# Tap matrices from unnormalized exponentials, transposes of two halves moved, five blocks in halves: a start-up change to a convolution and feed-forward kernel

## The chip, the cores and the metric

The kernel runs on one core of one Trainium2 chip. The metric is the device time of one execution in microseconds (us). Times are medians of several executions of one compiled kernel. PE is TensorE (PEld its weight loads), DVE is VectorE, ACT is ScalarE, POOL is GpSimd, and SP is the engine that issues DMAs.

## The reference

A causal depthwise convolution with softmax weights over 7 taps, then a two-layer feed-forward with leaky ReLU:

```python
w = np.exp(weight - weight.max(-1, keepdims=True))            # [8 heads, 7 taps]
w = w / (w.sum(-1, keepdims=True) + 1e-9)
# x: [8, 4096, 192], 24 columns to a head, padded with 6 zero rows in front
y = np.einsum('hk,bskhg->bshg', w, x_unfolded)                 # the convolution
h = y.reshape(32768, 192) @ w_in                               # 192 -> 2048
out = np.maximum(0.01 * h, h) @ w_out                          # 2048 -> 192
```

## The kernel before

Two batch rows are worked on side by side. Rows are taken in blocks of 512 positions (32 blocks), and the first `NHALF` blocks are cut in two. I call the pieces half 0, half 1 and so on, in order; `groups` lists them. While PE works on one group, DVE computes the convolution of the next group (21 instructions: 3 column chunks of 7 taps). The point at which the halves end and whole blocks of 512 begin I call the change of width, and DVE's lead is how far its convolutions run ahead of PE. For halves 0 and 1 PE computes two of the three chunks itself, by multiplying with diagonal "tap matrices", one for each tap and each of two bf16 parts of the weight (high and low).

```python
groups = [(b, h * HT, HT) for b in range(NHALF) for h in range(2)]     # NHALF = 3
groups += [(b, 0, ST) for b in range(NHALF, NBLK)]
...
# start: softmax, divided first, then split in two bf16 parts, then tap matrices
nc.vector.tensor_scalar_add(rsum, wraw[:, :, K : K + 1], 1e-9)
nc.vector.reciprocal(rsum, rsum)
nc.vector.tensor_mul(wk, wraw[:, :, 0:K], rsum.to_broadcast([128, NCH, K]))
nc.vector.tensor_copy(out=wkb, in_=wk)
...
# main loop: j is a step of two units; a unit is the first matmul for 2 (or 1) of 16 F-chunks
for j in range(steps):
    for u in range(2 * j, 2 * j + 2):
        mm1(grp, u)                          # first matmul, then ACT: leaky ReLU to g
        ...
    for _ in range(quota):
        mm2_slot(slot)                       # second matmul, lagging one group behind
    ...
    if i in (1, 2) and j == 0:
        transpose_first(i + 1)               # PE: transposes of the NEXT half's x
        evac_first(i + 1, nc.vector.tensor_copy, nc.vector.tensor_copy)
    for job in ahead[per * j : per * (j + 1)]:
        job()                                # DVE: convolution of the next group
    if i == 1 and j == 3:
        for e in range(2):
            cast_first(3, e, nc.vector.tensor_copy)
```

Only the first four halves are cast and transposed on the engines like this. All later blocks are cast by the load and transposed by a DMA.

Of the kernel before, what the change touches and what calls it, by code (L numbers as in the profile page):

```python
# [9 lines left out]
FP32 = mybir.dt.float32  # L10
BF16 = mybir.dt.bfloat16
# [3 lines left out]
def kernel(  # L15
# [8 lines left out]
    nc = tc.nc  # L24

    B, S, D = x.shape
    H, K = weight.shape
# [8 lines left out]
    NCH = D // CH  # L36
    ST = 512
# [5 lines left out]
    NBLK = (B // 2) * NB  # L43
    LAG = NFC + NFC // 2
    WQ = 4
    NHALF = 3
    NPEC = 2

    const_pool = ctx.enter_context(tc.tile_pool(name="const", bufs=1))
# [51 lines left out]
    def new_xt(rp):  # L101
        xt[rp] = xt_pool.tile([128, NCH, HALO + S], BF16, name="xt")
        nc.vector.memset(xt[rp][:, :, 0:HALO], 0.0)
# [3 lines left out]
    def load_first(q):  # L107
        t = stage_pool.tile([128, 2, HS, D], FP32, name="x_nat")
        for e in range(2):
            nc.sync.dma_start(  # L110
                out=t[:, e, :, :],
                in_=x[e, q * HT : (q + 1) * HT, :].rearrange("(c p) d -> p c d", p=128),
            )
        x_nat[q] = t

    def cast_first(q, e, copy):
        if q % 2 == 0 and e == 0:
            x_bf[q // 2] = xb_pool.tile([128, NCH, SUB, 2, CH], BF16, name="x_bf")
        h = q % 2
        copy(  # L120
            out=x_bf[q // 2][:, :, h * HS : (h + 1) * HS, e, :],
            in_=x_nat[q][:, e, :, :].rearrange("p s (c k) -> p c s k", c=NCH),
        )
# [3 lines left out]
    def transpose_first(q):  # L127
        ts = [
            psum_o.tile([128, HS, NCH, CH], BF16, name=f"ptr{i}", tag="po") for i in range(2)
        ]  # L130
        for s in range(HS):
            for c in range(NCH):
                for i in range(2):
                    ps = slice(i * CH, (i + 1) * CH)
                    nc.tensor.transpose(  # L135
                        out=ts[i][:, s, c, :],
                        in_=x_bf[q // 2][ps, c, (q % 2) * HS + s, :, :].rearrange(
                            "p e k -> p (e k)"
                        ),
                        identity=ident[ps, ps],  # L140
                    )
        ptr[q] = ts

    def evac_first(q, *copies):
        dst = xt[0][:, :, HALO + q * HT : HALO + (q + 1) * HT].rearrange(
            "p c (s i k) -> p i s c k", s=HS, i=2
        )
        for i, t in enumerate(ptr.pop(q)):
            copies[i](out=dst[:, i], in_=t)  # L149


    yt = {}
# [27 lines left out]

    def pe_conv_jobs(grp, c):

        blk, t0, T = grp
        acc = psum_o.tile([128, ST], FP32, name="acc", tag="po")
        jobs = []
        for k in range(K):
            for p in range(2):
                jobs.append(
                    lambda k=k, p=p: nc.tensor.matmul(  # L189
                        out=acc[:, :T], lhsT=diag[c][:, p, k, :],  # L190
                        rhs=xt[0][:, c, BASE + k + blk * ST + t0 : BASE + k + blk * ST + t0 + T],
                        start=(k == 0 and p == 0), stop=(k == K - 1 and p == 1),
                    )
                )
        return jobs, lambda copy: copy(out=yt[blk][:, c, t0 : t0 + T], in_=acc[:, :T])  # L195


    w9 = const_pool.tile([H, K + 1], FP32, name="w9")
    nc.scalar.dma_start(out=w9[:, 0:K], in_=weight)
    load_first(0)  # L200
    load_first(1)

    zero = const_pool.tile([128, ST], BF16, name="zero")
    nc.vector.memset(zero, 0.0)  # L204
    junk = const_pool.tile([128, 1], FP32)
    nc.vector.memset(junk, 0.0)  # L206
# [26 lines left out]
    def warm(n):  # L233
        for _ in range(n):
            nc.tensor.matmul(  # L235
                out=wa[:, 0, :], lhsT=zero[:, 0:128], rhs=zero, start=True, stop=True
            )


# [7 lines left out]
        out=w9[:, 0:K], in_=w9[:, 0:K], func=mybir.ActivationFunctionType.Exp,  # L247
        bias=nmax, scale=1.0, accum_out=w9[:, K : K + 1],
    )
    warm(6)  # L250
    wps = psum_h.tile([128, 2, ST], FP32, name="wps", tag="ph")
    for c in range(NCH):
        nc.tensor.matmul(  # L253
            out=wps[:, 0, c * (K + 1) : (c + 1) * (K + 1)],
            lhsT=sel[:, c, :, :].rearrange("h e k -> h (e k)"),
            rhs=w9, start=True, stop=True,
        )
    new_xt(0)
    cast_first(0, 0, nc.vector.tensor_copy)
    cast_first(0, 1, nc.scalar.copy)  # L260
    wraw = wps[:, 0, 0 : NCH * (K + 1)].rearrange("p (c k) -> p c k", c=NCH)
    rsum = const_pool.tile([128, NCH, 1], FP32)
    nc.vector.tensor_scalar_add(rsum, wraw[:, :, K : K + 1], 1e-9)
    nc.vector.reciprocal(rsum, rsum)
    wk = const_pool.tile([128, NCH, K], FP32, name="wk")
    nc.vector.tensor_mul(wk, wraw[:, :, 0:K], rsum.to_broadcast([128, NCH, K]))

    wkb = const_pool.tile([128, NCH, K], BF16, name="wkb")
    wkp = const_pool.tile([128, 2, NCH, K], FP32, name="wkp")
    nc.vector.tensor_copy(out=wkb, in_=wk)  # L270
    nc.vector.tensor_copy(out=wkp[:, 0], in_=wkb)  # L271
    nc.vector.tensor_sub(wkp[:, 1], wk, wkp[:, 0])


    transpose_first(0)
    warm(3)
    evac_first(0, nc.vector.tensor_copy, nc.scalar.copy)
    diag = [const_pool.tile([128, 2, K, 128], BF16, name=f"diag{c}") for c in range(NPEC)]
    for p in range(2):
        nc.vector.tensor_mul(  # L280
            diag[0][:, p],
            ident[:, None, :].to_broadcast([128, K, 128]),
            wkp[:, p, 0, :, None].to_broadcast([128, K, 128]),
        )
        for k in range(K):
            nc.scalar.activation(  # L286
                out=diag[1][:, p, k, :], in_=ident,
                func=mybir.ActivationFunctionType.Copy, scale=wkp[:, p, 1, k : k + 1],
            )
    cast_first(1, 1, nc.scalar.copy)  # L290
    load_first(2)
    jobs = conv_jobs(groups[0], range(NPEC, NCH))
    for c in range(NPEC):
        pe_jobs, evac_y = pe_conv_jobs(groups[0], c)
        for job in pe_jobs:
            job()
        if c == 0:
            for job in jobs:
                job()
            evac_y(nc.vector.tensor_copy)  # L300
        else:
            evac_y(nc.scalar.copy)
    cast_first(1, 0, nc.vector.tensor_copy)
    load_first(3)
    load_x(2)
    transpose_x(2)
# [89 lines left out]
    for i, grp in enumerate(groups):  # L396
        blk, t0, T = grp
        steps = T // 64
        if t0 == 0:
            g[blk] = g_pool.tile([128, NFC, 2, ST], BF16, name="g", tag="g")  # L400
        quota = (avail - slot) // steps

        if i == 0:
            ahead, pe_ahead = [], []
        else:
            ahead = conv_jobs(groups[i + 1]) if i + 1 < len(groups) else []
        per = -(-len(ahead) // (steps - 1)) if T == ST else -(-len(ahead) // steps)
        for j in range(steps):
            for u in range(2 * j, 2 * j + 2):
                mm1(grp, u)  # L410
                if i == 0 and u == 0:
                    transpose_first(1)
                    evac_first(1, nc.vector.tensor_copy, nc.vector.tensor_copy)
                    ahead = conv_jobs(groups[1], range(NPEC, NCH))
                    evacs = []
                    for c in range(NPEC):
                        pe_jobs, evac_y = pe_conv_jobs(groups[1], c)
                        pe_ahead += pe_jobs
                        evacs.append(evac_y)
                    per = len(ahead)  # L420
                if i == 0 and u >= 2:
                    n = -(-len(pe_ahead) // (8 - u))
                    for job in pe_ahead[:n]:
                        job()
                    pe_ahead = pe_ahead[n:]
            for _ in range(quota):
                mm2_slot(slot)
                slot += 1
            if i == 0 and j == 3:
                for evac_y in evacs:  # L430
                    evac_y(nc.vector.tensor_copy)
                for e in range(2):
                    cast_first(2, e, nc.vector.tensor_copy)
            if i in (1, 2) and j == 0:

                transpose_first(i + 1)
                evac_first(i + 1, nc.vector.tensor_copy, nc.vector.tensor_copy)
            for job in ahead[per * j : per * (j + 1)]:
                job()
            if i == 1 and j == 3:  # L440
                for e in range(2):
                    cast_first(3, e, nc.vector.tensor_copy)

            last_half = t0 + T == ST
            if j == steps // 4 and last_half:
                load_x(blk + 3)
            if j == steps // 2 and last_half and blk > 0:
                transpose_x(blk + 2)
        avail += 2 * T // 128 * NFC
# [37 lines left out]
```

## Time and profile before

| | before |
|---|---|
| time, median of 3 runs | 709.54 us |
| span of the profiled execution | 708.6 us |
| PE busy, share of the span | 98% |
| PE waiting for DVE's convolution in the main loop | 6.5 us, three waits |

The profile's part on the chain of waits follows the last instruction back to whatever released it. For the kernel before, by engine:

```profile
PE 90%; DVE 8%; issue 1%; ACT 0%; ACTq 0%
```

The 8% of DVE, about 57 us, lie within the first 89 us. Behind that the profile lists no wait of PE for the convolution. The prediction below shows the lines on waits and timeline.

### The profile page before, as it was taken

The page shows a single profiled execution, that of the slowest core. Times are in us where ns is not written, and L with a number is a line of the kernel's source. Part 1 is how long each engine was busy: PE and PEld are TensorE (multiplying, and loading weights), DVE is VectorE, ACT ScalarE, POOL GpSimd, SP SyncE. Part 2 cuts the span into 40 slices and gives each one's busy share as a digit, 9 for nine tenths or more (in the row PEclk, how much of TensorE's full clock was granted, in tenths as well). Part 3 has the DMA queues.
Part 4 walks back from the last instruction along what each step waited for, and adds up shares of the span by engine and source line. Part 5 has one row for each costly group of instructions (what it writes and reads, how often), then busy time and mean ns, then how long its engine had stood idle before and what let it go on. Part 6 is the DMA issues. An engine that isn't in the chain of part 4 may idle for free.

```text
span 708.6 us, 25496 instructions
## 1 busy us (share of the span) xinstructions
PE 694.9 (98%) x11527; PEld 609.1 (86%) x11527; DVE 537.1 (76%) x970; ACT 509.2 (72%) x558; POOL 142.0 (20%) x198
## 2 busy tenths in 40 slices
PE   8979999999999999999999999999999999999997
PEld 4879967888888888888888888888888888888887
DVE  5579996777778777778877777877777877777712
ACT  5757797777777777777777777777777777777770
POOL 7431150122221122222022222112222111000000
PEclk9999999999999999999999999999999999999999
DMA  9972674555653565664455655455576355222112
GB/s 177 119 76 50 83 86 69 79 74 75 81 85 65 84 70 73 91 80 74 76 74 75 80 81 86 66 78 76 72 92 80 64 86 69 52 63 58 46 36 68
DMA packets 184845, 54.35 MB, mean 77 GB/s; under 512 B 148384, under 2 KB 184736, under 8 KB 184736
## 3 DMA queue, kind: packets, MB, share of 16 engines
q0 software_dynamic: 98768, 14.17, 29.1%
q1 hardware_dynamic: 85952, 38.56, 23.7%
q8 instruction: 90, 1.47, 0.9%
q14 instruction: 19, 0.16, 0.1%
q10 hardware_dynamic: 16, 0.00, 0.0%
HBM read 29.88 MB, written 25.17 MB: 78 GB/s over the span
## 4 chain that ended last, share of the span: by engine, by line
PE 90%; DVE 8%; issue 1%; ACT 0%; ACTq 0%
PE po L348 45%; PE ph L328 43%; DVE yt L174 7%; PE acc L189 1%; DVE yt L168 1%; PE warm L235 0%; ACT g L335 0%; DVE xt L149 0%; PE wps L253 0%; DVE diag L280 0%; PE ptr L135 0%; DVE yt L195 0%; ACT yt L195 0%; DVE o_sb L387 0%; DVE zero L204 0%
## 5 line engine op out<-in xcount | busy, mean ns | idle before, releaser
L335 ACT ACTIVATE g<-ph 128x1024 bf16<-128x1024 f32 x512 | 496.6, 1021 | 176.2 <-PE ph L328 176.2
L174 DVE SCALAR_TENSOR_TENSOR yt<-xt,wk,yt 128x512 bf16<-128x512 bf16 (+1 forms) x606 | 431.8, 713 | 15.8
L348 PEld LDWEIGHTS <-g 64*128 64x128 bf16 (+1 forms) x8048 | 375.4, 94 | 30.8 <-ACT g L335 0.4
L328 PE MATMUL ph<-yt,w_in 64*128 64x512 bf16 (+1 forms) x3360 | 394.7, 359 | 7.4 <-DVE yt L174 6.5
L348 PE MATMUL po<-w_out,g 64*128 64x192 bf16 (+1 forms) x8048 | 400.9, 243 | 0.1
L328 PEld LDWEIGHTS <-w_in 64*128 64x128 bf16 x3360 | 244.9, 94 | 55.9 <-issue 12.1
L79 POOL DMA_DIRECT2D x_bf<-in_x_dram x180 | 133.7, 772 | 444.3 <-DMA xt<-x_bf 429.4
L387 DVE COPY o_sb<-po 128x192 f32<-128x192 f32 x232 | 83.0, 358 | 135.2 <-PE po L348 132.6
L168 DVE TENSOR_SCALAR yt<-xt,wk 128x512 bf16<-128x512 bf16 (+1 forms) x101 | 34.6, 343 | 0.1
L189 PE MATMUL acc<-xt,diag 128*128 128x256 bf16 x56 | 9.6, 325 | 1.4 <-DVE diag L280 1.4
L189 PEld LDWEIGHTS <-diag 128*128 128x128 bf16 x56 | 5.8, 114 | 5.4 <-DVE diag L280 2.6
L149 DVE COPY xt<-ptr 128x384 bf16<-128x384 bf16 x7 | 2.2, 352 | 7.8 <-PE ptr L135 7.8
L387 ACT COPY o_sb<-po 128x192 f32<-128x192 f32 x24 | 7.8, 327 | 0.3 <-PE po L348 0.3
L235 PE MATMUL warm<-zero 128*128 128x512 bf16 x9 | 4.2, 628 | 1.3 <-DVE junk L206 1.3
L223 POOL DMA_DIRECT2D w_in<-in_moe_w_in_dram x8 | 5.1, 643 | 0.0
L195 DVE CAST yt<-acc 128x256 bf16<-128x256 f32 x3 | 1.3, 422 | 4.8 <-PE acc L189 4.8
L286 ACT ACTIVATE diag<-ident,wkp 128x128 bf16<-128x128 bf16 x14 | 4.2, 386 | 0.2 <-DVE wkp L271 0.2
L235 PEld LDWEIGHTS <-zero 128*128 128x128 bf16 x9 | 1.0, 134 | 2.7 <-issue 1.4
L120 DVE CAST x_bf<-x_nat 128x384 bf16<-128x384 f32 x6 | 2.5, 450 | 1.0 <-DMA x_nat<-in_x_dram 1.0
L195 ACT CAST yt<-acc 128x256 bf16<-128x256 f32 x1 | 0.4, 372 | 3.0 <-PE acc L189 3.0
L240 ACT ACT_TABLE_LOAD x1 | 1.3, 1283 | 1.4 <-PEq L471 1.4
L280 DVE TENSOR_TENSOR diag<-ident,wkp 128x896 bf16<-128x896 bf16 x2 | 2.1, 1084 | 0.0
(28 smaller groups left out, 14.1 us busy)
## 6 DMA issues: line engine op xcount, KB each, us to landing
out_dram<-o_sb SPq DMA_DIRECT2D x128, 192.0 KB, 2.1
x_bf<-in_x_dram POOLq DMA_DIRECT2D x180, 64.0 KB, 3.2
x_nat<-in_x_dram SPq DMA_DIRECT2D x8, 192.0 KB, 3.8
w_in<-in_moe_w_in_dram POOLq DMA_DIRECT2D x8, 192.0 KB, 9.1
xt<-x_bf SPq DMA_TRANSPOSE x90, 2.4
w_out<-in_moe_w_out_dram POOLq DMA_DIRECT2D x1, 768.0 KB, 15.0
w<-in_weight_dram ACTq DMA_DIRECT2D x1, 0.2 KB
```

The costliest lines, as they stand in the source:

```text
L79: nc.gpsimd.dma_start(out=t[:, c, :, e, :], in_=src[2 * rp + e, :, :, c * CH : (c + 1) * CH],)
L120: copy(out=x_bf[q // 2][:, :, h * HS : (h + 1) * HS, e, :], in_=x_nat[q][:, e, :, :].rearrange("p s (c k) -> p c s k", c=NCH),)
L168: lambda s=src, d=dst, c=c: nc.vector.tensor_scalar_mul(d, s, wk[:, c, 0:1])
L174: lambda s=src, d=dst, c=c, k=k: nc.vector.scalar_tensor_tensor(out=d, in0=s, scalar=wk[:, c, k : k + 1], in1=d, op0=mybir.AluOpType.mult, ...
L189: lambda k=k, p=p: nc.tensor.matmul(out=acc[:, :T], lhsT=diag[c][:, p, k, :], rhs=xt[0][:, c, BASE + k + blk * ST + t0 : BASE + k + blk * ...
L223: nc.gpsimd.dma_start(out=w_in[e * CH : (e + 1) * CH, :, fs], in_=moe_w_in[:, fs].rearrange("(c p) f -> p c f", p=CH),)
L235: nc.tensor.matmul(out=wa[:, 0, :], lhsT=zero[:, 0:128], rhs=zero, start=True, stop=True)
L286: nc.scalar.activation(out=diag[1][:, p, k, :], in_=ident, func=mybir.ActivationFunctionType.Copy, scale=wkp[:, p, 1, k : k + 1],)
L328: nc.tensor.matmul(out=ph[:, e, i * T : (i + 1) * T], lhsT=w_in[ps, c, f * 128 : (f + 1) * 128], rhs=y[ps, c, t0 : t0 + T], start=(c == 0) ...
L335: act = nc.scalar.activation(out=g[blk][:, nf * u : nf * (u + 1), :, t0 : t0 + T], in_=ph.rearrange("p e (i t) -> p i e t", i=nf), func=my ...
L348: ins = nc.tensor.matmul(out=po[m], lhsT=g[b][ps, fc, e, s * 128 : (s + 1) * 128], rhs=w_out[ps, fc, :], start=(rt != 1 and fc == 0), stop ...
L387: copy(out=o_sb[:, n % 2, :], in_=po.pop(n))
```

## The change

Its intent is to make PE start its real work earlier and not wait for DVE in the first blocks. It has three parts, which I call **start**, **move** and **halves**.

```diff
 # start: tap matrices from the exponentials as they are; the divisor comes at evacuation
+    wkh = const_pool.tile([128, NCH, K], BF16, name="wkh")
+    wkl = const_pool.tile([128, NCH, K], FP32, name="wkl")
+    nc.vector.tensor_copy(out=wkh, in_=wraw[:, :, 0:K])
+    nc.vector.tensor_sub(wkl, wraw[:, :, 0:K], wkh)
...
+    diag_high(0)                 # DVE: high parts, one instruction for a chunk
+    diag_low(0, range(2))        # ACT: low parts, one instruction for a tap
...
-        return jobs, lambda copy: copy(out=yt[blk][:, c, t0 : t0 + T], in_=acc[:, :T])
+        return jobs, lambda scale: scale(yt[blk][:, c, t0 : t0 + T], acc[:, :T], rsum[:, c, :])
...
-    warm(6)                      # 128x512 on zeros, meant to raise PE's clock
+    warm(7)                      # 128x256 now; also 4 behind the weights' matmuls,
...                               # 3 behind the transposes and 3 behind each tap chain
 # move: order inside the loop
-                if i == 0 and u >= 2:            # taps of half 1 spread over six units
+                if i == 0 and u in (3, 5):       # in two runs of 14
...
-            if i in (1, 2) and j == 0:           # behind the first step of the half before
-                transpose_first(i + 1)
+            if i < 2 and j == 3:                 # one step earlier: in front of that step
+                transpose_first(i + 2)
...
 # halves
-    NHALF = 3
+    NHALF = 5
```

More of the change, by code (lines that the diff above doesn't have):

```diff
@@ L185, in pe_conv_jobs @@
         jobs = []
-        for k in range(K):
-            for p in range(2):
+        for p in range(2):
+            for k in range(K):
                 jobs.append(
@@ L194, in pe_conv_jobs @@
                 )
-        return jobs, lambda copy: copy(out=yt[blk][:, c, t0 : t0 + T], in_=acc[:, :T])
+        return jobs, lambda scale: scale(yt[blk][:, c, t0 : t0 + T], acc[:, :T], rsum[:, c, :])
     w9 = const_pool.tile([H, K + 1], FP32, name="w9")
-    nc.scalar.dma_start(out=w9[:, 0:K], in_=weight)
+    nc.sync.dma_start(out=w9[:, 0:K], in_=weight)
     load_first(0)
     load_first(1)
-    zero = const_pool.tile([128, ST], BF16, name="zero")
+    zero = const_pool.tile([128, HT], BF16, name="zero")
     nc.vector.memset(zero, 0.0)
@@ L235, in warm @@
             nc.tensor.matmul(
-                out=wa[:, 0, :], lhsT=zero[:, 0:128], rhs=zero, start=True, stop=True
+                out=wa[:, 0, 0:HT], lhsT=zero[:, 0:128], rhs=zero, start=True, stop=True
             )
@@ L257 @@
         )
+    warm(4)
     new_xt(0)
@@ L261, with diag_high, diag_low @@
     wraw = wps[:, 0, 0 : NCH * (K + 1)].rearrange("p (c k) -> p c k", c=NCH)
+    wkh = const_pool.tile([128, NCH, K], BF16, name="wkh")
+    wkl = const_pool.tile([128, NCH, K], FP32, name="wkl")
+    nc.vector.tensor_copy(out=wkh, in_=wraw[:, :, 0:K])
+    nc.vector.tensor_sub(wkl, wraw[:, :, 0:K], wkh)
+    diag = [const_pool.tile([128, 2, K, 128], BF16, name=f"diag{c}") for c in range(NPEC)]
+    def diag_high(c):
+        nc.vector.tensor_mul(
+            diag[c][:, 0],
+            ident[:, None, :].to_broadcast([128, K, 128]),
+            wkh[:, c, :, None].to_broadcast([128, K, 128]),
+        )
+    def diag_low(c, ks):
+        for k in ks:
+            nc.scalar.activation(
+                out=diag[c][:, 1, k, :], in_=ident,
+                func=mybir.ActivationFunctionType.Copy, scale=wkl[:, c, k : k + 1],
+            )
+    transpose_first(0)
+    warm(3)
+    diag_high(0)
+    diag_low(0, range(2))
+    evac_first(0, nc.vector.tensor_copy, nc.scalar.copy)
+    diag_low(0, range(2, K))
+    diag_high(1)
+    diag_low(1, range(K))
     rsum = const_pool.tile([128, NCH, 1], FP32)
@@ L266, with act_scale @@
     nc.vector.tensor_mul(wk, wraw[:, :, 0:K], rsum.to_broadcast([128, NCH, K]))
-    wkb = const_pool.tile([128, NCH, K], BF16, name="wkb")
-    wkp = const_pool.tile([128, 2, NCH, K], FP32, name="wkp")
-    nc.vector.tensor_copy(out=wkb, in_=wk)
-    nc.vector.tensor_copy(out=wkp[:, 0], in_=wkb)
-    nc.vector.tensor_sub(wkp[:, 1], wk, wkp[:, 0])
-    transpose_first(0)
-    warm(3)
-    evac_first(0, nc.vector.tensor_copy, nc.scalar.copy)
-    diag = [const_pool.tile([128, 2, K, 128], BF16, name=f"diag{c}") for c in range(NPEC)]
-    for p in range(2):
-        nc.vector.tensor_mul(
-            diag[0][:, p],
-            ident[:, None, :].to_broadcast([128, K, 128]),
-            wkp[:, p, 0, :, None].to_broadcast([128, K, 128]),
-        )
-        for k in range(K):
-            nc.scalar.activation(
-                out=diag[1][:, p, k, :], in_=ident,
-                func=mybir.ActivationFunctionType.Copy, scale=wkp[:, p, 1, k : k + 1],
-            )
-    cast_first(1, 1, nc.scalar.copy)
+    def act_scale(out, in_, scale):
+        nc.scalar.activation(
+            out=out, in_=in_, func=mybir.ActivationFunctionType.Copy, scale=scale
+        )
     load_first(2)
-    jobs = conv_jobs(groups[0], range(NPEC, NCH))
+    for job in conv_jobs(groups[0], range(NPEC, NCH)):
+        job()
     for c in range(NPEC):
@@ L296 @@
             job()
-        if c == 0:
-            for job in jobs:
-                job()
-            evac_y(nc.vector.tensor_copy)
-        else:
-            evac_y(nc.scalar.copy)
+        evac_y(act_scale)
+        warm(3)
     cast_first(1, 0, nc.vector.tensor_copy)
+    cast_first(1, 1, nc.vector.tensor_copy)
     load_first(3)
@@ L410 @@
                 mm1(grp, u)
-                if i == 0 and u == 0:
+                if i == 0 and u == 1:
                     transpose_first(1)
@@ L420 @@
                     per = len(ahead)
-                if i == 0 and u >= 2:
-                    n = -(-len(pe_ahead) // (8 - u))
-                    for job in pe_ahead[:n]:
+                if i == 0 and u in (3, 5):
+                    for job in pe_ahead[: 2 * K]:
                         job()
-                    pe_ahead = pe_ahead[n:]
+                    pe_ahead = pe_ahead[2 * K :]
             for _ in range(quota):
@@ L428 @@
                 slot += 1
-            if i == 0 and j == 3:
+            for job in ahead[per * j : per * (j + 1)]:
+                job()
+            if i == 0 and j == 2:
                 for evac_y in evacs:
-                    evac_y(nc.vector.tensor_copy)
+                    evac_y(nc.vector.tensor_scalar_mul)
                 for e in range(2):
                     cast_first(2, e, nc.vector.tensor_copy)
-            if i in (1, 2) and j == 0:
-                transpose_first(i + 1)
-                evac_first(i + 1, nc.vector.tensor_copy, nc.vector.tensor_copy)
-            for job in ahead[per * j : per * (j + 1)]:
-                job()
-            if i == 1 and j == 3:
+            if i == 1 and j == 2:
                 for e in range(2):
                     cast_first(3, e, nc.vector.tensor_copy)
+            if i < 2 and j == 3:
+                transpose_first(i + 2)
+                evac_first(i + 2, nc.vector.tensor_copy, nc.vector.tensor_copy)
             last_half = t0 + T == ST
```

## The prediction

> **What bounds the kernel now.** I read the page first, to see which engine fills the span.
>
> ```profile
> PE 694.9 (98%) x11527; PEld 609.1 (86%) x11527; DVE 537.1 (76%) x970; ACT 509.2 (72%) x558; POOL 142.0 (20%) x198
> PEclk9999999999999999999999999999999999999999
> ```
>
> PE is busy nearly always, so only two things can shorten the span: PE's own gaps, and stretches in which its work runs slowly. The waits of PE, next, name the gaps.
>
> ```profile
> PE ph L328 <- DVE yt L174: 6.5, 3, 2.8
> PE acc L189 <- DVE diag L280: 1.4, 2, 0.8
> ```
>
> Only 6.5 us in three waits belong to the main loop: the first matmul (L328) waits for the convolution on DVE (L174). Then the timeline of PE, to date them and see what follows each.
>
> ```profile
> 35.78 0.40 PE L328 MATMUL ph<-yt,w_in 64*128 64x256 bf16 x4
> 39.01 1.27 PE L328 MATMUL ph<-yt,w_in 64*128 64x256 bf16 x20 [2.83 <-DVE yt L174]
> 40.10 2.56 PE L348 MATMUL po<-w_out,g 64*128 64x192 bf16 x32
> ...
> 51.13 0.40 PE L328 MATMUL ph<-yt,w_in 64*128 64x256 bf16 x4
> 53.87 2.23 PE L328 MATMUL ph<-yt,w_in 64*128 64x256 bf16 x20 [2.34 <-DVE yt L174]
> 55.85 2.26 PE L348 MATMUL po<-w_out,g 64*128 64x192 bf16 x32
> 57.93 1.49 PE L328 MATMUL ph<-yt,w_in 64*128 64x256 bf16 x24
> 59.24 1.50 PE L348 MATMUL po<-w_out,g 64*128 64x192 bf16 x32
> ```
>
> The reader is to see that a gap costs twice. Behind each, 32 second matmuls take 2.56 or 2.26 us in place of 1.50; the windows view has the granted clock at 0.50 in 41 to 43 us and 54 to 56 us. Undisturbed, a step (24 first, 32 second matmuls) takes 2.63 us, so a half-block of four steps takes 10.52 (65.82 to 76.34). Half 2 took 14.86 (39.01 to 53.87), half 3 took 11.95 (53.87 to 65.82).
>
> Why is DVE late? Its timeline says:
>
> ```profile
> 25.08 0.86 DVE L120 CAST x_bf<-x_nat 128x384 bf16<-128x384 f32 x2
> 28.11 0.62 DVE L149 COPY xt<-ptr 128x384 bf16<-128x384 bf16 x2 [2.17 <-PE ptr L135]
> ...
> 42.98 0.62 DVE L149 COPY xt<-ptr 128x384 bf16<-128x384 bf16 x2 [3.36 <-PE ptr L135]
> 43.63 0.41 DVE L168 TENSOR_SCALAR yt<-xt,wk 128x256 bf16<-128x256 bf16 x1
> ```
>
> DVE sits idle for 2.17 and 3.36 us because the transposes (L135) stand behind a first and a second matmul in PE's order; the first matmul itself waits for DVE. It is a ring: PE waits for a convolution, DVE then waits for PE. The chain of waits agrees: from 29 us to 88.76 us it is almost only L174. So up to 88.76 us **DVE's chain is the bound**, from there on PE.
>
> **What the Trainium skill says.** "TensorE: Matmul & The Clock Gate", part 1, the HAM clock gate: PE starts at half clock, and windows of about 3.4 us decide whether it gets the full one. The trace agrees: one 128x256 tap matmul averages 417 ns in 10 to 12 us and 272 ns from 13.5 us, so the first full clock comes near 13.2 us. It differs on one size: gaps of 2.83 and 2.34 us were enough to lose it. "VectorE: DVE Perf Modes", the perf-mode tier table: fp32 from PSUM runs in the slowest mode for copy and scalar multiply alike, so the new evacuation with the divisor should cost DVE what the plain one did, 422 ns; the trace has only the plain one. "ScalarE: Activation LUTs", on what ACT_TABLE_LOAD costs: a pointer operand adds about 93 ns to an ACTIVATE. ACT's plain evacuation took 372 ns, so the scaled one is an estimate of 0.47 us from that page; no trace of before shows it.
>
> **The change part by part.**
>
> *Start.* Before, DVE runs six tiny instructions of about 0.18 us from 5.42 to 6.64 us, then both tap matrices of chunk 0; PE's first tap matmul is at 7.97, and 27 more end at 14.06. The first matmul's real start is 14.53. After, only two tiny ones precede the first tap matrix. The weights' load goes first on SP's queue, which should delay x by one issue, 0.46 us: casts at 3.8 and 4.3 us. The wps matmuls no longer wait for six 512-wide warm ones: 3.0 (sel is ready at 2.94) plus 1.45 gives 4.4. Then 0.4 for the bf16 high part and the rest, 1.04 for the first tap matrix (1084 ns with its latency), evacuation 0.35: taps from 6.4 us. At half clock, 27 matmuls before ran at about 213 ns each where cold, so chunk 0 ends at 6.4 + 14 x 0.213 = 9.4, three warm ones of 0.21 bring 10.0. ACT's fourteen low-part products at 0.3 us each (4.20 for fourteen) start at 4.9, have two casts or copies between, and end near 9.9: just in time. PE is then busy from 5.8 us, so I put full clock near 10 us; chunk 1 takes 14 x 0.109 = 1.5, to 11.5. ACT's scaled evacuation: 12.05. DVE's own chunk starts at 7.9 and takes 3.65: 11.55, beside it. The first unit of first matmuls thus ends at 12.5 instead of 15.25.
>
> *Half 0.* Eight units of 0.65, 28 taps x 0.109, transposes 0.35 and six changes of matmul shape at about 0.1: 9.4 us, PE-bound, to 21.9. Before it took from 14.53 to 24.63. The taps in two runs instead of six save some changes of shape. ACT's eight activations at 1.0 fit.
>
> *Transposes moved.* Both casts of half 2 come straight after the tap evacuations on DVE (about 21.4), the transposes on PE run 21.9 to 22.3, DVE's two copies to 22.95. Then DVE is unbroken: half 2's convolution is 9.97 us (60.37 to 70.34 for one), plus 0.86 for half 3's casts: 33.8. Half 3's transposes run on PE near 32.8, in front of the next first matmul; DVE copies to 34.45 and convolves to 44.4. PE: half 1 from 22.3, ready at 32.8, starts half 2's last chunk at about 33.9 instead of 39.01, half 3 at 44.6 instead of 53.87. The remaining gaps are about 1.0 and 0.2 us, under those that cost the clock, so I count no slow stretch.
>
> *Five blocks in halves.* A half gains DVE 10.52 - 9.97 = 0.55 us of lead. Six more until half 9 give 3.3 us. The first full-width convolution takes 14.95 us (six of 0.785, one of 0.27 for each of three chunks, 73.66 to 88.6). It ends at 44.4 + 6 x 9.97 + 14.95 = 119.2. PE would be ready at 44.6 + 7 x 10.52 = 118.3, so a wait of about 1 us stays at the change of width, as now (1.29). With three blocks the lead would be only 1.1 us and this wait about 3. ACT takes 16 more output copies of 0.33 us; it has 0.48 idle per step already with them. Two blocks in halves cost PE 2 x (21.04 - 20.92) = 0.24 us.
>
> *Sum.* Compare the start of block 6, with equally much second matmul left over. Before: 88.76 + 8 x 2.07 (reduced share) + 2 x 20.92 = 147.1. After: 119.3 + 16.55 = 135.8. Everything after is the same PE work. Gain 11.3: **709.54 - 11.3 = 698.2 us**, 1.6%.
>
> **The rivals.**
> First, *the cold start stays*: PE's clock rises only at about 12.6 us (two windows from 5.8). Then chunk 1 ends at 13.0, the first unit at 14.0 and all that follows 1.5 us later: 699.7. Speaking for it: before, PE was occupied from 1.26 to 7.2 us and still cold. Against: that stretch had wps matmuls and transposes in it, and 9 to 13 us of taps did raise the clock.
> Second, *the weights' landing takes over*. POOL's timeline shows when its queue came free:
>
> ```profile
> 11.93 0.74 POOL L79 DMA_DIRECT2D x_bf<-in_x_dram  x1 [0.87 <-DMA w_in<-in_moe_w_in_dram]
> 14.07 0.74 POOL L79 DMA_DIRECT2D x_bf<-in_x_dram  x1 [1.40 <-DMA w_in<-in_moe_w_in_dram]
> ...
> 23.47 3.71 POOL L79 DMA_DIRECT2D x_bf<-in_x_dram  x5 [4.30 <-DMA w_out<-in_moe_w_out_dram]
> ```
>
> By that w_out is there at 23.4 us (8.16 + 15.0 to landing), and the second matmul now wants it at 23.6; the second quarter of w_in is there at about 13.9 (read from the order of issues), wanted at 13.6. If either slips by 1 us, half 0 ends later and the sum is 699; a late w_out has a microsecond of slack, since DVE is the bound at half 2.
> Third, *the ring stays in part*: a gap over 2 us before half 2 or 3 would bring back a slow stretch of about 2 us besides, so 702 to 704. It would take DVE 1.3 us later than worked out.
> Fourth, *all PE loss vanishes*: the three waits, both slow stretches and 3 us of start together would be 6.5 + 4 + 3 = 13.5, so 696. That is still not 2%.
>
> **Range and chances.** Main line 698.2; the cold start and the weights add up to 1.5 each, the ring more; little can make it better than 696.3. Range 696.3 to 701.0. Faster by over 2% means under 695.35, a gain of 14.2, more than the fourth rival: 0.04. Slower by 2% has nothing for it: 0.01. Within 2%: 0.95.
>
> **What would show it.** In the profile after: the first L341 matmul near 12 us and half 1 near 22.3; DVE's waits for ptr falling from 7.8 us to under 2.5; PE's waits for yt from 6.5 to 2 to 3, with the longest at about 119 us; 32 second matmuls at 1.50 us everywhere before it, with no clock under 1.0 after 13 us; the first full-width unit at about 119. Wrong if half clock shows in 30 to 60 us, if PE waits for w_in or w_out by a microsecond, or if the wait at the change of width exceeds 2 us.

## The result, and the profile after

| | before | after |
|---|---|---|
| median (same rounds, 4 runs each) | 709.64 us | 699.42 us |
| lowest to highest | 709.53 to 710.04 | 699.01 to 699.55 |
| ratio | | 0.9854, interval 0.9837 to 0.9871 |
| span of the profiled execution | 708.6 us | 697.3 us |

A ratio is the mean time of one kernel's runs over that of the other's of the same rounds, so it is not quite the ratio of the medians quoted here. The result is 10.2 us or 1.5% faster, and inside the predicted range.

The page of the kernel after, busy time by engine and then the chain by engine:

```profile
PE 689.5 (99%) x11730; PEld 611.6 (88%) x11730; DVE 541.0 (78%) x995; ACT 512.2 (73%) x574; POOL 142.0 (20%) x198
...
PE 92%; DVE 4%; DMA 3%; ACT 0%; POOL 0%; issue 0%; POOLq 0%; ACTq 0%
```

DVE's share of the chain has halved. Part of that is only how the view goes back: it runs through PE from 44.7 to 104.5 us, but DVE too waits for nothing from 33.54 us until the first full-width convolution ends at 119.6, so DVE's chain still sets the change of width. The 3% of DMA are new: they are the landing of w_in and w_out. From the chain in order of time (start and duration):

```profile
2.90 6.14 DMA w_in<-in_moe_w_in_dram
...
9.33 14.18 DMA w_out<-in_moe_w_out_dram
```

So in this execution the loads are the bound up to 23.5 us, PE's work (with ACT's between 31.0 and 33.1) to 33.5, and only then DVE. In the second profiled execution of this kernel, changed_again, the chain has no load in it. The waits (total, times, longest, in us):

```profile
DVE xt L149 <- PE ptr L135: 1.8, 3, 0.9
...
PE ph L341 <- DVE yt L174: 1.4, 2, 0.9
...
PE ph L341 <- DMA w_in<-in_moe_w_in_dram: 0.4, 1, 0.4
```

DVE's wait for the transposes fell from 7.8 to 1.8 us, PE's wait for the convolution from 6.5 to 1.4. Some first matmuls now wait 0.4 us for w_in. The timeline of PE at the places where the gaps were (start and duration in us; L341 is the first matmul, L361 the second; idle time before it in brackets):

```profile
33.34 1.48 PE L341 MATMUL ph<-yt,w_in 64*128 64x256 bf16 x24
34.66 1.49 PE L361 MATMUL po<-w_out,g 64*128 64x192 bf16 x32
...
43.87 0.39 PE L341 MATMUL ph<-yt,w_in 64*128 64x256 bf16 x4
44.70 1.27 PE L341 MATMUL ph<-yt,w_in 64*128 64x256 bf16 x20 [0.44 <-DVE yt L174]
45.79 1.50 PE L361 MATMUL po<-w_out,g 64*128 64x192 bf16 x32
...
118.12 0.61 PE L341 MATMUL ph<-yt,w_in 64*128 64x512 bf16 x4
119.66 1.04 PE L341 MATMUL ph<-yt,w_in 64*128 64x512 bf16 x8 [0.93 <-DVE yt L174]
```

Half 2 starts at 33.34 without a gap (before: four matmuls at 35.78, the rest at 39.01 behind 2.83 us), half 3 at 44.70 behind 0.44 us (before: 53.87 behind 2.34 us). The second matmuls behind them take 1.50 us, so the clock was kept. At the change to full width 0.93 us of waiting is left, against 1.29 in the kernel before:

```profile
88.76 1.04 PE L328 MATMUL ph<-yt,w_in 64*128 64x512 bf16 x8 [1.29 <-DVE yt L174]
```

And the start of the loop, same columns (L135 is the transpose of half 2):

```profile
10.88 1.69 PE L341 MATMUL ph<-yt,w_in 64*128 64x256 bf16 x24
...
13.68 1.48 PE L341 MATMUL ph<-yt,w_in 64*128 64x256 bf16 x23 [0.38 <-DMA w_in<-in_moe_w_in_dram]
...
21.11 0.34 PE L135 MATMUL ptr<-ident,x_bf 64*128 64x64 bf16 x12
...
23.55 1.31 PE L361 MATMUL po<-w_out,g 64*128 64x192 bf16 x14
```

The first matmul starts at 10.88 us, against 14.00 before. The third unit then waits for the second quarter of w_in (13.68), and the first second matmul starts at 23.55, when w_out is there (its load, issued at 9.3, took 14.2 us to land). That is 1.82 us behind the start of half 1, against 1.57 in changed_again (22.34 to 23.91), which had w_out in time; so w_out cost about 0.25 us here.

Where did the time come from? Read at equal progress, the start of block 6: the first matmul of that block begins at 146.90 us before and at 135.85 after:

```profile
146.90 1.51 PE L328 MATMUL ph<-yt,w_in 64*128 64x512 bf16 x12
```

```profile
135.85 1.58 PE L341 MATMUL ph<-yt,w_in 64*128 64x512 bf16 x12
```

That is 11.05 of the 11.3 us between the two profiled spans; the other 0.25 us come later.

### The profile page after: what moved, and what is told of

Read it like the earlier page. It is cut to its first block, busy times and chain, and to the rows that moved or that the text cites. A ratio compares the mean times of both kernels' runs of the same rounds, so it can differ in the third digit from the quotient of the medians.

```text
span 697.3 us, 25946 instructions
## 1 busy us (share of the span) xinstructions
PE 689.5 (99%) x11730; PEld 611.6 (88%) x11730; DVE 541.0 (78%) x995; ACT 512.2 (73%) x574; POOL 142.0 (20%) x198
## 4 chain that ended last, share of the span: by engine, by line
PE 92%; DVE 4%; DMA 3%; ACT 0%; POOL 0%; issue 0%; POOLq 0%; ACTq 0%
PE po L361 47%; PE ph L341 45%; DVE yt L174 3%; DMA w_out<-in_moe_w_out_dram 2%; DMA w_in<-in_moe_w_in_dram 1%; ACT g L348 0%; DVE yt L168 0%; POOL sel L214 0%; DVE xt L149 0%; POOL sel L212 0%; PE ptr L135 0%; DVE o_sb L400 0%; POOL ident masks.py:199 0%; ACT o_sb L400 0%; POOL ident masks.py:197 0%
## 5 line engine op out<-in xcount | busy, mean ns | idle before, releaser
L174 DVE SCALAR_TENSOR_TENSOR yt<-xt,wk,yt 128x512 bf16<-128x512 bf16 (+1 forms) x642 | 439.7, 685 | 17.4
L361 PE MATMUL po<-w_out,g 64*128 64x192 bf16 (+1 forms) x8048 | 397.8, 243 | 0.1
L361 PEld LDWEIGHTS <-g 64*128 64x128 bf16 (+1 forms) x8048 | 372.1, 94 | 28.8 <-issue 0.4
L341 PE MATMUL ph<-yt,w_in 64*128 64x512 bf16 (+1 forms) x3552 | 391.9, 347 | 2.5 <-DVE yt L174 1.4
L341 PEld LDWEIGHTS <-w_in 64*128 64x128 bf16 x3552 | 249.1, 94 | 48.0 <-issue 5.4
L400 DVE COPY o_sb<-po 128x192 f32<-128x192 f32 x216 | 77.3, 358 | 127.2 <-PE po L361 124.8
L400 ACT COPY o_sb<-po 128x192 f32<-128x192 f32 x40 | 13.1, 327 | 0.0
L236 PE MATMUL warm<-zero 128*128 128x256 bf16 x20 | 4.5, 372 | 1.1 <-DVE junk L207 1.1
L282 ACT ACTIVATE diag<-ident,wkl 128x128 bf16<-128x128 bf16 x14 | 4.3, 391 | 0.1
L274 DVE TENSOR_TENSOR diag<-ident,wkh 128x896 bf16<-128x896 bf16 x2 | 2.2, 1082 | 0.0
L135 PEld LDWEIGHTS <-x_bf 64*128 64x128 bf16 x48 | 1.2, 101 | 0.9 <-issue 0.8
L135 PE MATMUL ptr<-ident,x_bf 64*128 64x64 bf16 x48 | 1.7, 202 | 0.2 <-ACT o_sb L400 0.2
## 6 DMA issues: line engine op xcount, KB each, us to landing
w_out<-in_moe_w_out_dram POOLq DMA_DIRECT2D x1, 768.0 KB, 14.2
```

What stands on the lines that cost most here:

```text
L135: nc.tensor.transpose(out=ts[i][:, s, c, :], in_=x_bf[q // 2][ps, c, (q % 2) * HS + s, :, :].rearrange("p e k -> p (e k)"), identity=ident ...
L174: lambda s=src, d=dst, c=c, k=k: nc.vector.scalar_tensor_tensor(out=d, in0=s, scalar=wk[:, c, k : k + 1], in1=d, op0=mybir.AluOpType.mult, ...
L236: nc.tensor.matmul(out=wa[:, 0, 0:HT], lhsT=zero[:, 0:128], rhs=zero, start=True, stop=True)
L282: nc.scalar.activation(out=diag[c][:, 1, k, :], in_=ident, func=mybir.ActivationFunctionType.Copy, scale=wkl[:, c, k : k + 1],)
L341: nc.tensor.matmul(out=ph[:, e, i * T : (i + 1) * T], lhsT=w_in[ps, c, f * 128 : (f + 1) * 128], rhs=y[ps, c, t0 : t0 + T], start=(c == 0) ...
L361: ins = nc.tensor.matmul(out=po[m], lhsT=g[b][ps, fc, e, s * 128 : (s + 1) * 128], rhs=w_out[ps, fc, :], start=(rt != 1 and fc == 0), stop ...
```

## The experiments

**Theory.** Up to the change of width the end is set by one chain through DVE. The start begins it earlier, the move takes PE out of it, and five halves give DVE the lead for the first full-width convolution. **Rivals:** the start is hidden behind the landing of the weights; the number of halves is of no matter; and what PE loses at half clock behind each gap is a sum of its own, which comes back whole.

The three parts were put on and taken off one by one. With before and after, six more kernels give all eight combinations. Each change is one part of the diff shown above. Start and move each bundle several edits (in start also the load of the softmax weights on another queue and the warm-ups, in move the taps in two runs and the earlier casts and transposes); apart from the warm-ups they were not taken apart. All results were correct.

| kernel | start | move | halves | median us | range us | ratio to before (95% interval) |
|---|---|---|---|---|---|---|
| before | | | | 709.6 to 710.4 | 709.33 to 711.54 | 1 |
| only_start | x | | | 709.87 | 707.07 to 710.47 | 0.9988 (0.9965 to 1.0011) |
| only_move | | x | | 703.55 | 702.88 to 705.38 | 0.9911 (0.9893 to 0.9928) |
| only_halves | | | x | 708.44 | 707.99 to 708.76 | 0.9975 (0.9959 to 0.9992) |
| start_move | x | x | | 702.20 | 701.31 to 703.10 | 0.9888 (0.9873 to 0.9903) |
| start_halves | x | | x | 706.40 | 706.08 to 706.57 | 0.9946 (0.9931 to 0.9960) |
| move_halves | | x | x | 701.73 | 701.22 to 701.87 | 0.9879 (0.9864 to 0.9894) |
| after | x | x | x | 699.42 | 699.01 to 699.55 | 0.9854 (0.9837 to 0.9871) |
| changed_again (after, other rounds) | x | x | x | 699.53 | 699.04 to 700.05 | 0.9850 (0.9836 to 0.9863) |

The kernel before is given by its medians in the several rounds, on three different chips.

**only_start.**

> The kernel before with the new start alone (unnormalized tap matrices, scaled evacuation, warm-ups), old order in the loop, three blocks in halves. Theory (one chain through the ring of PE and DVE): the first unit of first matmuls ends near 11.8 us in place of 15.25, but the second quarter of w_in lands at 13.7, so half 1 starts about 2.4 us earlier, and all of it reaches the end: 707.2 us (706.5 to 708). PE's waits for yt stay at 6 to 7 us and the slow stretches at 40 and 54 us stay. Rival (the start is hidden behind the weights' landing or swallowed by the later waits): 709.0 to 709.6.

Measured 709.87 us: nothing in the median, a miss, though one run took 707.07. The timeline of PE shows where it went (columns as above):

```profile
37.06 2.09 PE L341 MATMUL ph<-yt,w_in 64*128 64x256 bf16 x20 [2.69 <-DVE yt L174]
...
87.50 1.04 PE L341 MATMUL ph<-yt,w_in 64*128 64x512 bf16 x8 [3.17 <-DVE yt L174]
88.36 1.34 PE L361 MATMUL po<-w_out,g 64*128 64x192 bf16 x16
89.46 2.71 PE L341 MATMUL ph<-yt,w_in 64*128 64x512 bf16 x12
```

Half 1 starts at 23.34 us against 25.21, so the start's gain enters the loop. It is 1.95 us at half 2 (37.06 against 39.01) and 1.26 us at the full width (87.50 against 88.76). But PE's gap there grew from 1.29 to 3.17 us, and it now costs the clock: 16 second matmuls take 1.34 us in place of 0.84, 12 first ones 2.71 in place of 1.72. By block 6 the gain is gone: its first unit begins at 147.06 us, against 146.90.

**start_fill** and **before_fill** hold the clock in the gaps, to test that account and the rival on slow stretches:

```diff
         ph = psum_h.tile([128, 2, ST], FP32, name="ph", tag="ph")
+        if u == 0 and grp in (groups[2], groups[3], groups[6]):
+            for _ in range(20):
+                nc.tensor.matmul(
+                    out=ph[:, 0, 0:HT], lhsT=zero[:, 0:128], rhs=zero[:, 0:HT],
+                    start=True, stop=True,
+                )
```

> The kernel before with 20 matmuls on zeros (about 2.2 us, overwritten by the real ones) put in front of the first matmuls of half 2, half 3 and the first full-width block, that is into the three gaps, so that PE's clock isn't lost; nothing else. Theory (DVE's chain is the bound up to the change of width, and a slow stretch reaches the end only as far as it delays the transposes of half 3): the slow stretches vanish, DVE enters the full width about 1.1 us earlier, PE waits longer there: 708.4 us (707.6 to 709.0). Rival (what PE loses in slow stretches, some 4 us, comes back whole, as the fourth rival of the prediction summed it): 705 to 706. Rival (the gaps are not what costs the clock): slow stretches stay and 709.6 or more.

> The kernel with the new start alone, plus the same 20 filling matmuls in its three gaps. The new start alone gave nothing in the median (709.87, but 707.07 in one run of four), and its profiled run has a slow stretch behind the gap at the change of width (88 to 92 us). Theory: the start's gain does reach DVE's chain (convolution for the full width ready 1.2 us earlier), and is given back by a longer gap there and the clock lost behind it; with the clock held it shows: 706.3 us (705.6 to 707.3), runs within 1 us of each other. Rival (the start's gain is swallowed before the ring, by the weights' landing): no better than the fill alone in the kernel before.

before_fill took 709.29 us against 710.22 for the kernel before in the same rounds (ratio 0.9988, interval 0.9973 to 1.0003, which holds 1). start_fill took 707.21 (0.9956, interval 0.9939 to 0.9972), its runs within 0.7 us. The timeline of PE in before_fill (L334 first, L354 second matmul):

```profile
24.44 1.38 PE L334 MATMUL ph<-yt,w_in 64*128 64x256 bf16 x22 [0.30 <-DVE yt L195]
...
38.31 1.27 PE L334 MATMUL ph<-yt,w_in 64*128 64x256 bf16 x20 [0.51 <-DVE yt L174]
39.40 1.50 PE L354 MATMUL po<-w_out,g 64*128 64x192 bf16 x32
...
52.40 1.27 PE L334 MATMUL ph<-yt,w_in 64*128 64x256 bf16 x20 [0.40 <-DVE yt L174]
...
87.57 1.04 PE L334 MATMUL ph<-yt,w_in 64*128 64x512 bf16 x8 [0.82 <-DVE yt L174]
```

The 32 second matmuls are at 1.50 us again, in place of 2.56, so an idle gap was what cost the clock. Yet the full width begins only 1.19 us earlier (87.57 against 88.76), and not all of that is the filling's: half 1 began at 24.44 against 25.21 and half 2 at 38.31 against 39.01, because the taps of the start happened to run faster in this execution. The distance to the kernel before grew from 0.70 us at half 2 to 1.47 at half 3 (52.40 against 53.87), so the filling brought some 0.8 us; 0.28 were lost again by the full width, as much as one scalar multiply on DVE took too long (0.55 us at 68.88 in place of 0.28). The agreement of 1.19 with the 1.1 of the theory is therefore partly luck. The rival that some 4 us come back whole (705 to 706) falls all the more. The median lies 0.3 us above the range that I gave; that of start_fill is inside its range. The difference of start_fill to before_fill, 2.1 us, is the gain of the start when the clock is held. So the account of only_start holds: the start's gain was real, and was given back, in the execution profiled, at the change of width by a longer gap and the clock behind it.

**only_move** and **start_move.**

> The kernel before with the new order in the loop alone (tap matmuls of half 1 in two runs, casts and transposes of halves 2 and 3 moved), old start, three blocks in halves. Theory: both gaps before halves 2 and 3 fall under 1 us and the clock stays full; but DVE then enters half 5 with a lead of only about 1.1 us in place of 3.3, so the wait at the change to full width grows from 1.29 us to about 3.3 and may bring one slow stretch of up to 1.7 us: 703.0 to 704.5 us. Rival (the ring was most of the loss and the change of width costs no more than now): 701 to 702. Rival (the transposes were not the cause of DVE's lateness): 708 to 709.

> The changed kernel with three blocks in halves in place of five. Theory: DVE's lead at the change of width is 1.1 us in place of 3.3, so the wait there grows from 0.93 us to about 3.1, 1.8 us net of the dearer halves, and a gap of 3 us costs the full clock in most runs, up to 1.7 us more: 701.2 to 703.2 us, with granted clock 0.5 behind about 80 us. Rival (the number of halves does nothing, the other two parts are the whole gain): 699.2 to 699.6.

Measured 703.55 and 702.20 us, both as the theory had it. The first full-width matmul of only_move, then (in a fence of its own) that of start_move:

```profile
82.06 1.04 PE L328 MATMUL ph<-yt,w_in 64*128 64x512 bf16 x8 [2.94 <-DVE yt L174]
```

```profile
79.75 1.04 PE L341 MATMUL ph<-yt,w_in 64*128 64x512 bf16 x8 [2.95 <-DVE yt L174]
```

The wait at the change of width is 2.9 us where there are only six halves, as worked out from a lead of 1.1 us. In both profiled executions the clock was kept behind it. start_move was profiled in its fastest run (701.31 us); its slowest took 703.10. That the slower ones lost the clock there was not looked at. The record only lists a mean granted clock of 0.998 for the two slower runs of start_move (702.70 and 703.10) and 1.000 for the two faster; in only_move the fastest run (702.88) has 0.998 too, so this does not settle it.

**only_halves.**

> The kernel before with five blocks in halves in place of three, nothing else. Theory: DVE's lead at half 5 is already 3.3 us, because PE lost time in the ring; four more halves add 2.2, so the 14.95 us of the first full-width convolution fit and the wait at the change (1.29, with the restart 1.9 us) goes; two blocks in halves cost 0.24: 707.9 us (707.4 to 708.6). Rival (halves are as good at any time, and this part is worth as much here as in the whole change, 2 us or more): 707.5 or less with the wait for yt at 80 us or later still there in the rest.

Measured 708.44 us (ratio 0.9975): as the theory had it. PE waits for the convolution only twice, before halves 2 and 3, and no more at the change of width. Its gain of some 1.6 us here is smaller than the 2.8 us that it brings on top of the other two parts (702.20 to 699.42).

**start_halves** and **move_halves.**

> The changed kernel with the old order in the loop put back (taps spread, transposes behind the second matmul), new start and five blocks in halves kept. Theory: the ring stays, with gaps of about 2.7 us before halves 2 and 3 and a slow stretch in one or both; with nine halves DVE's lead nearly covers the full-width convolution, so a wait of 1.5 us at most is left at the change: 707.3 us (706.5 to 708.2). Rival (five halves and the new start together suffice, the move is not needed): under 702.

> The changed kernel with the old start put back; new order in the loop and five blocks in halves kept. Theory: DVE's chain begins 2.3 us later than in the whole change and nothing makes that up, since DVE is the bound until the full width: 701.7 us (701.2 to 702.4), with a wait of about 1 us at the change and no slow stretch. Rival (the new start is hidden behind the landing of w_in and w_out): 699.4 to 700.0.

Measured 706.40 and 701.73 us. The second is right on the theory, with a wait of 0.92 us at the change. The first is 0.9 us better than the centre and 0.1 below the range: only one of its two gaps cost the clock in the profiled execution.

From the eight, two readings of each part: alone, start 0.1, move 6.4, halves 1.6 us; taken out of the whole change, start 2.3 (701.73 - 699.42), move 7.0 (706.40 - 699.42), halves 2.8. The sum of the parts alone is 8.1 us, less than the 10.2 of the whole: what the start and the move bring forward is partly lost at the change of width unless the halves give DVE the lead there.

**no_warm.** The changed kernel without the warm-ups, save the first seven:

```diff
-    warm(4)
...
-    warm(3)
...
-        warm(3)
```

> The changed kernel without its warm-up matmuls on zeros, save the first seven: the four behind the weights' matmuls, the three behind the first transposes and the three behind each tap chain are taken away. Theory: the clock then rises near 10 to 13 us in place of 7.5, both tap chains run at half clock, the first unit of first matmuls ends 1 to 1.5 us later; of that 0.65 is hidden by the wait for w_in's second quarter and 0.3 by w_out: 700.0 us (699.6 to 701.0). Rival (the warm-ups do nothing, or all is hidden behind the weights): 699.2 to 699.6.

Measured 700.29 us, 0.8 us more than the changed kernel, so the time is as expected. But the profile doesn't show the mechanism that I gave. The average of a tap matmul, read in steps of 0.5 us, falls to 272 ns (full clock) only after 10.5 us without the warm-ups. In the changed kernel it does so after 8 us in one profiled execution and after 10 us in the other (changed_again). No-warm's half 1 starts at 21.95 us; in changed_again it starts at 22.34, later. (The clock is read from the matmuls here: the windows view gives 1.00 for the first 11 us of the changed kernel, although tap matmuls took about 418 ns in 7 to 7.5 us.) What is later in no_warm is w_out:

```profile
24.08 1.31 PE L358 MATMUL po<-w_out,g 64*128 64x192 bf16 x14 [0.38 <-DMA w_out<-in_moe_w_out_dram]
```

By the start of block 6 no_warm is 0.83 us behind changed_again (137.17 against 136.34). Of this, 0.17 us is there at the first second matmul (24.08 against 23.91). Most of the rest stands on DVE, where three scalar multiplies of the convolution took 0.63, 0.63 and 0.58 us (at 34.73, 81.97 and 102.25) and their counterparts 0.45, 0.47 and 0.28. So the cost of 0.8 us in the median stands, on different chips and with ranges that overlap (699.88 to 700.36 against 699.04 to 700.05), but in the executions profiled it is not the clock's. Why such a multiply is slow was not tested, and that the warm-ups raise the clock earlier is not shown.

**six** and **six_wout4.** One more block in halves, and then also w_out loaded in four pieces:

```diff
-    NHALF = 5
+    NHALF = 6
...
-    nc.gpsimd.dma_start(out=w_out, in_=moe_w_out.rearrange("(c p) d -> p c d", p=128))
+    for q in range(4):
+        cs = slice(q * NFC // 4, (q + 1) * NFC // 4)
+        nc.gpsimd.dma_start(out=w_out[:, cs, :],
+            in_=moe_w_out.rearrange("(c p) d -> p c d", p=128)[:, cs, :])
```

> The changed kernel with six blocks in halves in place of five. Theory: two more halves give DVE 1.1 us of lead, which covers the wait at the change of width (0.93 us); the dearer halves cost 0.12: 0.8 us faster than the changed kernel, 698.6 us (698.3 to 699.0), no wait for yt over 0.5 us. Rival (the wait moves elsewhere, or the output copies on ACT get in the way): 699.2 or more.

> As the one with six blocks in halves, and w_out loaded in four pieces in place of one, so that the first second matmuls need only a quarter of it. Theory: PE's wait for w_out at 23.2 to 23.5 us in the changed kernel goes (0.36 us), half 1 ends that much earlier and, DVE being the bound behind it, it reaches the end in full or in part: 698.3 us (697.9 to 698.6). Rival (PE would wait as long elsewhere, or three more load issues delay the loads of x): no better than six alone.

Measured 698.61 us (698.08 to 699.56) and 697.83 us (697.44 to 698.85). The first full-width unit of six, then of six_wout4:

```profile
139.04 1.68 PE L341 MATMUL ph<-yt,w_in 64*128 64x512 bf16 x12
```

```profile
139.00 1.47 PE L346 MATMUL ph<-yt,w_in 64*128 64x512 bf16 x12
```

Twelve matmuls in one piece: the wait of 0.93 us at the change of width has gone, all but 0.2 us inside the unit of six. The time of six is the one expected. Of six_wout4, PE's second matmuls start at 23.11 us, straight behind the first ones, where they started at 23.55 in the changed kernel; the gain over six in the profiled spans is 0.3 us (696.4 to 696.1), in the medians 0.8. The runs of the two overlap, so that the four pieces add to six is not shown. In the profiles DVE's copies for half 3 come 0.56 us earlier (33.11 against 33.67), but half 3 only 0.04 (44.54 against 44.58): two scalar multiplies took 0.56 and 0.67 us there, and 0.42 and 0.28 in six. The median of six_wout4 lies 0.1 below the range expected. **six_wout4 beats both kernels:** all its five runs lie under all nine of the changed kernel (699.01 and more). The intervals of their ratios to the kernel before, 0.9812 to 0.9840 and 0.9837 to 0.9871 (again 0.9836 to 0.9863), just overlap, because the kernel before itself varies.

**changed_again.**

> The changed kernel once more, unaltered, because the kernel before has drifted from 709.6 to 710.4 us between the rounds, which is as much as the warm-ups (700.29 without them, against 699.42 measured earlier) and the six halves (698.61) are worth. If the drift is common to all kernels: about 700.1 us, and then the warm-ups are worth 0.2 us, the six halves 1.5. If the drift is in the kernel before alone (its slow stretches fall differently): 699.4 us, and the warm-ups are worth 0.9 and the six halves 0.8, as worked out.

Measured 699.53 us, so the changed kernel did not drift along, and the comparisons above stand on 699.4 to 699.5. Why the kernel before differs between the rounds, which ran on different chips, stays open: over these nine runs its slowest (711.33 us) has the lowest mean granted clock, 0.993, but its fastest (709.33) has 0.995 and another at 709.95 has 0.998.

## Why the prediction was right

- **The bound.** That "DVE's chain is the bound" up to the change of width, and PE from there on, is borne out by the eight combinations, by before_fill (some 2.9 us of slow PE work behind the first two gaps removed, some 0.8 gained by it in the profile) and by the start of block 6, behind which only 0.25 us changes. In the kernel after it holds from 33.54 us; before that the chain is that of the loads and of PE, as shown above.
- **Start.** Predicted, the first unit ends at 12.5 us. ACT takes up its result at 11.96, so it was some 0.6 us better; the clock rose near 7.7 us in that execution, not near 10. In the other profiled execution it rose near 9.6 us and the loop began at 11.88. The scaled evacuation on ACT took 0.46 to 0.47 us, as estimated; on DVE 0.48 in place of the 0.42 assumed.
- **Half 0 and the weights.** The second rival came true in part: 0.38 us of waiting for w_in and about 0.25 for w_out. Half 1 starts at 21.73 us, predicted 22.3. The microsecond of slack that the prediction gave a late w_out was not there: half 3's transposes stand behind half 1 in PE's order, and DVE waited 0.51 us for them.
- **Transposes moved.** Half 2 starts without the gap of about 1.0 us that was expected, half 3 at 44.70 us, predicted 44.6. To this tenth it is luck, since several small terms cancel: DVE's convolution of half 2 begins 0.8 us earlier than worked out (22.14 against 22.95) and the casts of half 3 take 0.2 less, but DVE waits 0.51 us for half 3's transposes (which waited for an output copy on ACT, 0.24 us), and two scalar multiplies of the convolution took 0.59 and 0.66 us in place of 0.28. PE's waits for the convolution come to 1.4 us, under the 2 to 3 predicted. Two of these lines:

```profile
33.54 0.62 DVE L149 COPY xt<-ptr 128x384 bf16<-128x384 bf16 x2 [0.51 <-PE ptr L135]
...
40.86 0.66 DVE L168 TENSOR_SCALAR yt<-xt,wk 128x256 bf16<-128x256 bf16 x1
```

- **Five blocks in halves.** The full width starts at 119.66 us behind 0.93, predicted 119.3 behind about 1. With three blocks the wait is 2.95, predicted about 3.
- **Sum.** The start of block 6 was put at 147.1 and 135.8 us; it was at 146.90 and 135.85. The gain there is 11.05, not the 11.3 worked out; that the profiled spans differ by 11.3 to the tenth is luck, since 0.25 of it comes later. The term that was mis-sized is the base it was taken from: the trace is of an execution of 710.32 us, and I subtracted its gain from the median of 709.54, which is 0.8 us faster. The execution profiled after (699.01) is also the fastest of its four, 0.4 under their median. With the medians the gain is 10.2, and 699.42 in place of 698.2.
- **First rival, the cold start:** it had 1.5 us between an early and a late clock. Two profiled executions with the clock up near 7.7 and 9.6 us differ by 0.5 us in span (697.3 and 697.8), because the early one waits 0.38 us for w_in and about 0.25 for w_out. **Fourth rival:** it summed waits, slow stretches and start to 13.5 us. before_fill shows that the slow stretches do not add up like this.

## What to carry to other kernels

When two engines wait for each other in turn, the waits of the slower-looking one are effects: follow both timelines, find what the other engine waits for, and take that out of the ring. A gain at the head of such a chain is worth only what the next tight place lets through, so test a part inside the whole change as well as alone: the start was worth nothing by itself and 2.3 us in company. And subtract a gain read from a trace from the time of that very execution, not from the median.

## What the Trainium skill lacked or had wrong

- "TensorE: Matmul & The Clock Gate", part 1 and its practical advice on idle gaps (none longer than about 3 to 3.4 us): here gaps of 2.34 and 2.69 us cost the clock, while gaps of 2.79, 2.94 and 2.95 us did not in the executions profiled. That fits the page's statement that the window is free-running, and not a limit on length alone.
- The same page gives the cost of lost clock as half the throttled time. Here holding the clock through the gaps brought some 0.8 us in the profile, although 32 second matmuls behind one gap alone had lost 1.06 us and a second such group 0.76: where another engine's chain is the bound, the page's sum is an upper bound.
- The same page, part 1, says the number of cold matmuls varies from run to run. The runs agree: with the same kernel the clock rose near 7.7 us in one execution and near 9.6 us in another; the time moved by 0.5 us.
- "VectorE: DVE Perf Modes", the perf-mode tier table, puts copy and scalar multiply from PSUM in one class: 422 ns for the plain evacuation of 128x256 and 483 ns with a scalar read for each partition, so 61 ns more, which the table does not tell.
- "SBUF — State Buffer", who interferes with whom, says that DVE in its two-port modes and GpSimd shut each other out. Scalar multiplies of 0.59 and 0.66 us in place of 0.28 stood in stretches where POOL issued loads of x (23.8 to 27.5 and 33.3 to 42.2 us), which would fit. In the profiles of before, after, changed_again, no_warm and six_wout4 all 16 multiplies of over 0.4 us between 20 and 140 us start while POOL issues such loads, but others in the same stretches took no more than usual (after, 37.53 us: 0.30); no run here separated it.
